# Performer attention and an MLP on one core: loads dealt in halves, omega on ScalarE's queue, and a few splits moved between VectorE and GpSimd

## The chip, the cores and the metric

The kernel runs on one core of a Trainium2 chip, the other cores idle. The metric is the device time of one execution in microseconds. Before and after are compared by the median of several executions; the profile comes from one more execution, whose own time is given below.

## The reference

```python
scale = 1.0 / np.sqrt(np.sqrt(D))             # D = 64; batch 8, heads 8, seq 576, 128 features
def phi(x):
    h = np.einsum('bhsd,md->bhsm', x, omega) - np.sum(x * x, -1, keepdims=True) / 2
    return np.exp(h - h.max(-1, keepdims=True)) / np.sqrt(m)
q_p, k_p = phi(q * scale), phi(k * scale)
kv, z = einsum('bhsm,bhsd->bhmd', k_p, v), k_p.sum(2)
attn = einsum('bhsm,bhmd->bhsd', q_p, kv) / (einsum('bhsm,bhm->bhs', q_p, z)[..., None] + 1e-6)
x = attn.transpose(0, 2, 1, 3).reshape(8, 576, 512)
u = x + (x.transpose(0, 2, 1) @ U @ V).transpose(0, 2, 1)      # mixing along the sequence, rank 32
out = u + np.maximum(u @ w_ch1, 0) @ w_ch2                     # 512 -> 2048 -> 512
```

U, V and the two weights are 64-bit floats, and the kernel decodes them on the chip. The 4608 rows of u make nine chunks of 512.

## The kernel before, in words

**Attention** runs in 16 rounds of 9 steps. Rounds come from 16 units of two batches by two heads; from round 1 on a round has two parts, one of keys and one of queries, and one step handles 128 positions of both. Each part needs a tile `kt` or `qt` of 128 by 1152 numbers, loaded in eight DMAs of 72 KB: `load(0)` brings the first half (four DMAs), `load(1)` the second. A part is turned by VectorE in three transposes of 384 columns (`turn`, L643, one per three steps), split into a high part on ScalarE (`high`, L647) and a remainder on GpSimd (`low`, L651), then projected on TensorE in three matmuls (L771 to L773). VectorE takes the maxima (`peak`, L779), ScalarE the exponentials (L786). TensorE then adds keys into `p_kv` (L683), or transposes queries (L709), which are copied out (`eT`, L714) and multiplied with `kv` (L729, L722). The program is written as a loop over steps with delays by stage (`DELAY`); a scheduler orders each engine's instructions, except where `keep_in_program_order` (K) fixes them.

All loads but a few stand on SyncE's queue, SP. Queue SP takes them in order. At the start omega comes through GpSimd's queue (tile `once`), is scaled and transposed (L838, L840) and split into `omh` and `oml`, without which no projection begins. Twelve matmuls on a tile of zeros (L819) stand on TensorE at the start.

**The decoder** (`decoding`) runs beside the attention and turns U, V and w_ch1 into 32-bit floats: ScalarE (L141, L144), three instructions on VectorE (L159, L160, L163, the `slots`) and an addition on GpSimd (L184). For each half of a group of w_ch1, `Half` then makes four sums (L269) and splits seven operands into high and low parts (L273, L278) for a seven-product matrix scheme; groups 0 and 1 are made during the attention on GpSimd, groups 2 and 3 later.

**Mixing** (`mixing`) runs beside the attention for three pairs of batches and after it for the last: rows are split on ScalarE and GpSimd (L427, L429) and multiplied (L474, L442).

**The MLP** starts inside the last mixing: `early` prepares chunk 0 of u, `guest` chunk 1 (transposes L598, sums L531, splits L536 and L540), and `unit` issues the seven products (L1028), with additions on VectorE (L1014) between them. `BEGIN`, `PACE` and two tuples in the loop over `begun` say at which places the other work is dealt in. The second matmul of the MLP (L1409) follows from about 674 us to the end.

## Time and profile before

| | us |
|---|---|
| three timed executions | 1023.04, 1036.34, 1041.23 |
| their median | 1036.34 |
| the profiled execution | 1022.2 |
| its span, first to last instruction | 1020.3 |
| TensorE busy in the span | 1002.5 |
| VectorE, ScalarE, GpSimd busy | 844.5, 614.6, 516.2 |
| mean granted clock of TensorE | 0.997 |

Busy time is the time in which an engine has an instruction under way. A busy TensorE is not TensorE at its peak: a matmul's record covers its latency, and matmuls overlap. The profiled execution lies beside the fastest of the timed ones.

### The profile page before, as it was taken

Reading aid. Unit: us, or ns where it says so; the run is one execution under the profiler, and the core shown is the slowest. Engines: PE = TensorE matmul, PEld = TensorE weight load, DVE = VectorE, ACT = ScalarE, POOL = GpSimd, SP = SyncE. Lnnn points to the kernel's source line nnn. Section 1 sums busy time; section 2 is a strip of 40 time slices with the busy share of each in tenths; the row PEclk is TensorE's granted clock in tenths of the full one; section 3 lists DMA queues with packets and bytes.
Section 4 is the critical chain, followed back from the end, with each engine's and each line's share of the span. In section 5 each row is a group of like instructions: output and inputs, shape, how many; then the busy total and the mean of one; then the engine's idle time right before and its main releaser. Section 6 shows DMA issues by size and latency. Waiting matters only on the chain.

```text
span 1020.3 us, 23875 instructions
## 1 busy us (share of the span) xinstructions
PE 1002.5 (98%) x8497; PEld 980.9 (96%) x8497; DVE 844.5 (83%) x1507; ACT 614.6 (60%) x1483; POOL 516.2 (51%) x453
## 2 busy tenths in 40 slices
PE   8999999999999999999999999999999999999998
PEld 7899999999997999999999999999999999999998
DVE  4699898898899796766567565779999999999995
ACT  5889989989885557446355354665444454454442
POOL 4446966867536353323415314525756646646543
PEclk9899999999999999999999999999999999999999
DMA  7688588587444785888679768874555455455451
GB/s 141 137 164 157 115 197 161 112 188 145 88 105 113 214 202 144 225 243 207 179 204 238 183 178 273 258 234 155 176 169 204 146 176 177 145 176 176 145 177 51
DMA packets 380518, 175.51 MB, mean 172 GB/s; under 512 B 275552, under 2 KB 353376, under 8 KB 375920
## 3 DMA queue, kind: packets, MB, share of 16 engines
q1 hardware_dynamic: 378000, 173.67, 64.3%
q8 instruction: 67, 1.10, 0.5%
q10 hardware_dynamic: 2368, 0.30, 0.2%
q14 instruction: 51, 0.42, 0.1%
q0 software_dynamic: 32, 0.03, 0.0%
HBM read 109.97 MB, written 63.96 MB: 170 GB/s over the span
## 4 chain that ended last, share of the span: by engine, by line
PE 58%; DMA 1%; DVE 0%; issue 0%; ACT 0%; DVEq 0%
PE p_q L1409 10%; PE p_p L1409 10%; PE p_n L1409 7%; PE p_n L1028 7%; PE p_p L1028 5%; PE p_q L1028 5%; PE p_kv L1409 5%; PE p_kv L1028 4%; PE p_m L1028 3%; PE p_m L1409 2%; DMA raw<-in_moe_w_ch_dram 1%; DVE g L1014 0%; DMA g<-g 0%; ACT g L1010 0%; DVE u L1334 0%
## 5 line engine op out<-in xcount | busy, mean ns | idle before, releaser
L786 ACT ACTIVATE e<-p_p,nm 128x128 f32<-128x128 f32 x576 | 166.4, 397 | 24.9 <-DVE nm L779 15.9
L1247 ACT CAST gh<-gs 128x512 fp32r<-128x512 f32 x140 | 86.8, 623 | 150.4 <-DVE gs L1219 82.9
L1219 POOL TENSOR_TENSOR gs<-graw 128x512 f32<-128x512 f32 x66 | 108.5, 1654 | 125.2 <-DMA graw<-g 72.0
L1010 ACT ACTIVATE g<-g 128x512 f32<-128x512 f32 x105 | 66.4, 634 | 148.0 <-DVE g L1014 91.7
L651 POOL TENSOR_TENSOR xl<-xT,xh 128x384 fp32r<-128x384 f32 x96 | 97.5, 1033 | 99.9 <-ACT xh L647 82.8
L1254 DVE TENSOR_TENSOR gl<-gs,gh 128x512 fp32r<-128x512 f32 x140 | 132.9, 955 | 7.7 <-ACT gh L1247 6.8
L779 DVE TENSOR_REDUCE nm<-p_p 128x4 f32<-128x512 f32 x144 | 98.1, 683 | 27.4 <-ACT e L786 10.3
L184 POOL TENSOR_TENSOR wf<-wf,low 128x512 int32<-128x512 int32 (+2 forms) x35 | 44.0, 1257 | 130.0 <-ACT g L1010 71.8
L771 PE MATMUL p_p<-omh,xh 128*128 128x256 f32 x288 | 93.2, 324 | 1.9 <-ACT e L786 1.6
L1334 POOL TENSOR_TENSOR u<-u,p 128x256 f32<-128x256 f32 x72 | 80.9, 1153 | 24.8 <-DVE u L1334 22.4
L1254 DVE TENSOR_TENSOR gl<-graw,gh 128x512 fp32r<-128x512 f32 x107 | 83.1, 800 | 3.1 <-ACT gh L1247 3.1
L772 PE MATMUL p_p<-oml,xh 128*128 128x256 f32 x288 | 81.5, 283 | 0.0
L773 PE MATMUL p_p<-omh,xl 128*128 128x256 f32 x288 | 81.4, 283 | 0.0
L1409 PE MATMUL p_p<-wh,gh 128*128 128x256 f32 x288 | 79.5, 276 | 0.0
L1409 PE MATMUL p_p<-wl,gh 128*128 128x256 f32 x288 | 79.5, 276 | 0.0
L1409 PE MATMUL p_p<-wh,gl 128*128 128x256 f32 x288 | 79.5, 276 | 0.0
L1247 ACT CAST gh<-graw 128x512 fp32r<-128x512 f32 x107 | 63.7, 621 | 25.6 <-PE p_n L1409 4.9
L1409 PE MATMUL p_q<-wh,gl 128*128 128x256 f32 x276 | 76.3, 276 | 0.0
L1409 PE MATMUL p_q<-wh,gh 128*128 128x256 f32 x276 | 76.2, 276 | 0.0
L1409 PE MATMUL p_q<-wl,gh 128*128 128x256 f32 x276 | 76.2, 276 | 0.0
L729 PE MATMUL p_n<-kv,eT 128*128 128x65 f32 x512 | 73.2, 272 | 2.9 <-ACT eT L714 1.9
L729 PEld LDWEIGHTS p_n<-kv,eT 128*128 128x128 f32 x512 | 68.3, 194 | 6.2 <-ACT eT L714 2.4
(291 smaller groups left out, 3935.8 us busy)
## 6 DMA issues: line engine op xcount, KB each, us to landing
g<-g SPq DMA_DIRECT2D x282, 128.0 KB, 2.6
graw<-g SPq DMA_DIRECT2D x35, 1024.0 KB, 5.2
raw<-in_moe_w_ch_dram SPq DMA_DIRECT2D x23, 512.0 KB, 4.7
u_dram<-ut SPq DMA_DIRECT2D x36, 256.0 KB, 2.5
u<-u_dram SPq DMA_DIRECT2D x36, 256.0 KB, 2.6
out_dram<-u SPq DMA_DIRECT2D x36, 256.0 KB, 2.5
kt<-in_k_dram SPq DMA_DIRECT2D x120, 72.0 KB, 2.5
qt<-in_q_dram SPq DMA_DIRECT2D x120, 72.0 KB, 2.5
```

The costliest lines, as they stand in the source:

```text
L651: nc.gpsimd.tensor_tensor(out=self.xl[-1], in0=self.turned, in1=f32(self.xh[-1]), op=ALU.subtract)
L729: nc.tensor.matmul(pn[:, h, :], eT[:, h, :], kv[:, h, s // 5, :], start=True, stop=True)
L771: nc.tensor.matmul(o, part.xh[g][:, ts], oh, start=True, stop=False)
L772: nc.tensor.matmul(o, part.xh[g][:, ts], ol, start=False, stop=False)
L773: nc.tensor.matmul(o, part.xl[g][:, ts], oh, start=False, stop=True)
L779: nc.vector.tensor_reduce(out=self.nm[:, :n], in_=self.pp[:, :n], axis=AX.X, op=ALU.max, negate=True)
L786: nc.scalar.activation(out=self.e[:, j, :], in_=self.pp[:, j, :], func=AF.Exp, bias=self.nm[:, j : j + 1])
L1028: K(nc.tensor.matmul(p[:, f, :], x[:, k, fs], y[:, k, :], start=first, stop=(k == 1 and y is ul), skip_group_check=True,))
L1219: K(engine.tensor_tensor(out=to, in0=self.val[x], in1=self.val[y], op=op))
L1247: K(nc.scalar.copy(out=h, in_=v))
L1254: K(nc.vector.tensor_tensor(out=l, in0=v, in1=f32(h), op=ALU.subtract))
L1409: K(nc.tensor.matmul(acc[bank][:, half, :], x[:, ks], y[:, f, :], start=(now.s == 0 and k == 0 and half == 0 and x is h and y is wh), stop ...
```

## The change

It does six things. Omega is loaded through ScalarE's queue, ahead of everything else there, and three of the four first-half loads of the second key part follow it on that queue (four of four stood there before); the fourth goes to SP. From round 2 on, the first halves of keys and queries are issued before the second halves. In round 0, the second transpose of the second part stands after the step's maxima. Eight GpSimd instructions on weights (the first sum and one early split of each half of groups 0 and 1) are made to wait for the decoder's latest VectorE slot. Some splits and sums change engine: split 3 of groups 2 and 3, splits 4 and 6 and one sum of `guest` go from VectorE to GpSimd, split 2 of `early` and one row split of the last mixing go from GpSimd to VectorE. And the tables that deal the MLP's other work change a little.

```diff
+    ahead_of = []
+    def behind(inst):
+        if ahead_of:
+            tc.add_manual_dep(
+                inst.ins, ahead_of.pop().ins.name,
+                mybir.DependencyInfo(mybir.DependencyClass.Sync, mybir.DependencyReason.SCHED_ONLY),
+            )
+        return inst
...
-                    tc.keep_in_program_order(slot())
+                    step = tc.keep_in_program_order(slot())
+                    if j < 2 and i < fine < 99:
+                        ahead_of[:] = [step]
...
-            self.sums.tensor_tensor(out=to, in0=self.v[x], in1=self.v[y], op=op)
+            made = self.sums.tensor_tensor(out=to, in0=self.v[x], in1=self.v[y], op=op)
+            if self.sums is nc.gpsimd:
+                behind(made)
...
-            engine = nc.vector if self.g >= EARLY_GROUPS and (0, 1, 0, 1, 0, 1, 0)[i] else self.lows
+            engine = nc.vector if self.g >= EARLY_GROUPS and (0, 1, 0, 0, 0, 1, 0)[i] else self.lows
...
-                rest = nc.vector if last and t not in (0, 1, 2, 3, 4, 5, 6, 7) else nc.gpsimd
+                rest = nc.vector if last and t not in (1, 2, 3, 4, 5, 6, 7) else nc.gpsimd
...
-                (queue or nc.sync).dma_start(
+                (nc.scalar if 2 * h + a < aside else nc.sync).dma_start(
...
-    nc.gpsimd.dma_start(out=once, in_=omega)
+    nc.scalar.dma_start(out=once, in_=omega)
+    keys[0].load(0)
+    keys[1].load(0, 3)
+    for p in keys:
+        p.load(1)
     nc.vector.memset(warm, 0.0)
     K(nc.scalar.activation(out=warm, in_=warm, func=AF.Exp))
-    keys[0].load(0)
-    keys[1].load(0, nc.scalar)
-    for p in keys:
-        p.load(1)
...
                 new[0].load(0)
-                if r:
-                    new[0].load(1)
             if t == 1:
                 new.append(Queries(r + last, 1))
                 new[1].load(0)
                 if r == 0:
                     for p in keys[:2]:
                         p.load_values(1, "t")
-                    new[0].load(1)
+                new[0].load(1)
                 new[1].load(1)
...
-                0, ahead, first, lows=(VE, VE, G_, G_, G_, G_, G_,), sums=(VE, G_, VE, VE,), ...
+                0, ahead, first, lows=(VE, VE, VE, G_, G_, G_, G_,), sums=(VE, G_, VE, VE,), ...
...
-    BEGIN = (3, 5, 6, 9, 11, 13, 14, 16, 17, 18, 19)
+    BEGIN = (3, 5, 6, 8, 11, 13, 14, 16, 17, 18, 19)
-    guest = prepare(1, ..., lows=(VE, VE, VE, VE, VE, VE, VE,), pool=tp, sums=(VE, G_, G_, G_,))
+    guest = prepare(1, ..., lows=(VE, VE, VE, VE, G_, VE, G_,), pool=tp, sums=(G_, G_, G_, G_,))
-    PACE = {2: (0, 1, 1, 0, 1, 2, 1), 3: (3, 3, 3, 3, 5, 3, 0), 4: (2, 1, 2, 1, 2, 4, 2), 5: (1, 1, 2, 1, 1, 1, 2)}
+    PACE = {2: (0, 1, 1, 0, 1, 2, 1), 3: (3, 3, 4, 3, 5, 3, 0), 4: (1, 1, 2, 1, 2, 4, 2), 5: (2, 1, 1, 1, 1, 1, 2)}
...
-        for _ in range((1, 1, 1, 1, 1, 1, 1)[i]):
+        for _ in range((1, 1, 1, 2, 1, 1, 1)[i]):
```

On the queue SP, the loads issued during round 1 (keys of unit 3 and queries of unit 1 for round 2, then the loads of V, values, and the loads for round 3) stood so before:

```order
L623 DMA kt<-in_k_dram 32x18x32 x8
L623 DMA qt<-in_q_dram 32x18x32 x8
L382 DMA raw<-in_moe_V_dram 32x576 x4
L665 DMA vt_134<-in_v_dram 128x4x64 x2
L670 DMA vm_135<-in_v_dram 64x2x64
```

and stand so after (line 638 is line 623 of before, L397 is L382, L680 is L665, L685 is L670):

```order
L638 DMA kt<-in_k_dram 32x18x32 x4
L638 DMA qt<-in_q_dram 32x18x32 x4
L638 DMA kt<-in_k_dram 32x18x32 x4
L638 DMA qt<-in_q_dram 32x18x32 x4
L397 DMA raw<-in_moe_V_dram 32x576 x4
L680 DMA vt_134<-in_v_dram 128x4x64 x2
L685 DMA vm_135<-in_v_dram 64x2x64
```

The four first-half loads of the queries moved ahead of the four second-half loads of the keys; what follows them is in the same order.

On ScalarE at the start of the program, the rows before were these (the tile `qt` holds the second key part here):

```order
L623 DMA qt<-in_k_dram 32x18x32
L811 ACT_TABLE_LOAD
L811 ACTIVATE warm<-warm 128x1
L623 DMA qt<-in_k_dram 32x18x32 x3
L843 CAST omh<-p_q 64x128 x2
```

and are these after:

```order
L824 DMA once<-in_omega_dram 128x64
L638 DMA qt<-in_k_dram 32x18x32 x3
L830 ACT_TABLE_LOAD
L830 ACTIVATE warm<-warm 128x1
L858 CAST omh<-p_q 64x128 x2
```

Omega took the first place, one key load left for SP, where it stands fifth, and the table load moved behind the DMAs.

On GpSimd in round 4 of the attention, where the first half of weight group 0 is made, with each row's semaphore waits (`ml` is a split of the mixing, `xl` a remainder of the attention), the rows before were:

```order
L184 TENSOR_TENSOR wf<-wf,low 128x512 [waits DVE_49]
L269 TENSOR_TENSOR ws<-wf 128x256 [waits Pool_49]
L429 TENSOR_TENSOR ml<-x,mh 128x512 [waits Activation_49]
L269 TENSOR_TENSOR wf<-wf 128x256 [waits Pool_49]
L269 TENSOR_TENSOR ws<-ws,wf 128x256
L429 TENSOR_TENSOR ml<-x,mh 128x512 [waits Activation_49]
L651 TENSOR_TENSOR xl<-xT,xh 128x384 [waits PE_49,Activation_49] x2
```

and after (L195 is L184, L444 is L429, L666 is L651, L280 is L269):

```order
L195 TENSOR_TENSOR wf<-wf,low 128x512 [waits DVE_49]
L444 TENSOR_TENSOR ml<-x,mh 128x512 [waits Activation_49] x2
L666 TENSOR_TENSOR xl<-xT,xh 128x384 [waits PE_49,Activation_49] x2
L280 TENSOR_TENSOR ws<-wf 128x256 [waits DVE_49,Pool_49]
L444 TENSOR_TENSOR ml<-x,mh 128x512 [waits PE_49,Activation_49]
L280 TENSOR_TENSOR wf<-wf 128x256 [waits Pool_49]
L280 TENSOR_TENSOR ws<-ws,wf 128x256
```

The first sum of the weights moved behind two splits of the mixing and two of the attention, and it waits for VectorE now. Eight such waits are new on GpSimd: one at the first sum and one at an early split of each of four halves.

## Rows read from the trace of the kernel before

**Rows 1.** Stretches of the span; by engine busy us and (instructions), granted clock, DMA share.

```profile
100.00:200.00 100.00, 98.89 (x813) 94.20 (x811) 89.89 (x218) 92.46 (x297) 80.81 (x83) 1.00 0.72 149
...
300.00:400.00 100.00, 96.38 (x767) 91.54 (x765) 86.87 (x160) 59.36 (x132) 48.44 (x43) 1.00 0.66 163
400.00:460.00 60.00, 59.04 (x512) 58.49 (x511) 40.27 (x61) 29.31 (x52) 18.35 (x15) 1.00 0.84 228
...
700.00:800.00 100.00, 100.00 (x885) 100.00 (x884) 99.18 (x140) 44.19 (x80) 63.13 (x46) 1.00 0.50 166
```

**Rows 2.** Waits of TensorE: who waited for whom, us in total, times, longest.

```profile
PE p_n L729 <- ACT eT L714: 1.9, 3, 1.2
...
PE py L474 <- POOL ml L429: 1.4, 3, 0.9
...
PE p_n L1028 <- DVE g L1014: 1.1, 2, 0.8
PE p_kv L1028 <- DVE g L1014: 0.9, 1, 0.9
```

**Rows 3.** Timeline around 42 us: start, us, engine, instruction, [idle before, releaser].

```profile
38.00 4.22 SPq L623 DMA_DIRECT2D qt<-in_q_dram  x8
...
39.24 0.15 DVE L739 TENSOR_SCALAR rec<-p_n 128x4 f32<-128x4 f32 x1
...
42.14 0.58 DVE L643 STREAM_TRANSPOSE xT<-qt 128x384 f32<-128x384 f32 x1 [2.74 <-DMA qt<-in_q_dram]
...
43.59 0.66 PE L729 MATMUL p_n<-kv,eT 128*128 128x65 f32 x4 [1.23 <-ACT eT L714]
...
45.66 1.12 PE L729 MATMUL p_n<-kv,eT 128*128 128x65 f32 x4 [0.51 <-DVE eT L714]
```

**Rows 4.** Stretches around the same place, columns as in rows 1.

```profile
42.00:44.40 2.40, 1.01 (x8) 0.73 (x6) 2.26 (x7) 1.19 (x4) 0.99 (x1) 0.99 0.80 143
44.40:51.20 6.80, 6.28 (x28) 5.91 (x29) 4.47 (x12) 5.37 (x18) 3.54 (x4) 0.50 0.68 146
51.20:60.00 8.80, 8.80 (x83) 8.80 (x81) 8.18 (x19) 6.62 (x24) 1.97 (x2) 1.00 0.71 116
```

**Rows 5.** Maxima on VectorE, one per step: ns min/median/max, first and last start.

```profile
L779 DVE TENSOR_REDUCE nm<-p_p x144: 652/691/693, 12.2 to 307.5; 128x4 f32<-128x512 f32 x144
```

**Rows 6.** The queue SP, timeline: two rows of its first 60 us.

```profile
32.48 5.42 SPq L623 DMA_DIRECT2D kt<-in_k_dram  x8
...
52.61 5.68 SPq L623 DMA_DIRECT2D qt<-in_q_dram  x8
```

**Rows 7.** The tile qt until 60 us: ns to issue a load, us to its landing.

```profile
L623 SPq DMA_DIRECT2D qt<-in_q_dram x24: 443/496/1901, 14.6 to 57.8; - x24
...
DMA to landing us min/median/max: 2.2/2.4/4.2
```

**Rows 8.** Timeline of the start, columns as in rows 3.

```profile
0.75 0.43 ACTq L623 DMA_DIRECT2D qt<-in_k_dram  x1
...
1.27 0.68 POOL L809 DMA_DIRECT2D once<-in_omega_dram  x1 [0.81 <-POOLq L1460]
...
4.67 0.30 DVE L838 TENSOR_SCALAR om<-once 128x64 f32<-128x64 f32 x2 [2.65 <-DMA once<-in_omega_dram]
...
6.82 0.58 DVE L643 STREAM_TRANSPOSE xT<-kt 128x384 f32<-128x384 f32 x1
```

**Rows 9.** Splits of line L278 by engine, 300 to 440 us: ns min/median/max.

```profile
L278 POOL TENSOR_TENSOR wl<-wf,wh x14: 737/742/1187, 348.3 to 400.4; 128x256 fp32r<-128x256 f32 x14
...
L278 DVE TENSOR_TENSOR wl<-ws,wh x6: 410/421/1284, 349.4 to 390.7; 128x256 fp32r<-128x256 f32 x6
```

**Rows 10.** Splits of line L540 on VectorE, 300 to 440 us, columns as in rows 9.

```profile
L540 DVE TENSOR_TENSOR wl<-uT,wh x4: 685/692/926, 341.1 to 347.4; 128x512 fp32r<-128x512 f32 x4
```

**Rows 11.** Timeline at 319 us, two splits that began together.

```profile
319.31 5.74 POOL L540 TENSOR_TENSOR ul<-x,uh 128x512 fp32r<-128x512 f32 x4 [1.02 <-ACT uh L536]
319.36 1.80 DVE L540 TENSOR_TENSOR u<-x,u 128x512 fp32r<-128x512 f32 x1
```

More of the change, by code (lines that the diff above doesn't have):

```diff
@@ L276, in low @@
             h, l = (x[:, self.half, :] for x in operand(self.g, i))
-            engine = nc.vector if self.g >= EARLY_GROUPS and (0, 1, 0, 1, 0, 1, 0)[i] else self.lows
-            K(engine.tensor_tensor(out=l, in0=self.v[LEFT[i]], in1=f32(h), op=ALU.subtract))
+            engine = nc.vector if self.g >= EARLY_GROUPS and (0, 1, 0, 0, 0, 1, 0)[i] else self.lows
+            made = K(engine.tensor_tensor(out=l, in0=self.v[LEFT[i]], in1=f32(h), op=ALU.subtract))
+            if engine is nc.gpsimd:
+                behind(made)
             ready.add((self.g, self.half, i))
@@ L614, in performer_mlp_kernel, with blocks @@
     ))
-    def blocks(src, raw, unit, j, queue=None):
+    def blocks(src, raw, unit, j, aside=0):
         pair, hp = unit
@@ L634, in __init__, with load @@
             self.xh, self.xl = [], []
-        def load(self, j, queue=None):
-            blocks(self.src, self.raw, self.unit, j, queue)
+        def load(self, j, aside=0):
+            blocks(self.src, self.raw, self.unit, j, aside)
         def turn(self):
@@ L895, in performer_mlp_kernel @@
             early = prepare(
-                0, ahead, first, lows=(VE, VE, G_, G_, G_, G_, G_,), sums=(VE, G_, VE, VE,), temps=lambda: next(aside).rearrange("p (k t) -> p k t", k=2)
+                0, ahead, first, lows=(VE, VE, VE, G_, G_, G_, G_,), sums=(VE, G_, VE, VE,), temps=lambda: next(aside).rearrange("p (k t) -> p k t", k=2)
             )
@@ L912, in performer_mlp_kernel @@
                 p.copy(st.s)
-        for st in at("turn1"):
-            for p in st.group(1):
-                p.turn()
+        if s != G:
+            for st in at("turn1"):
+                for p in st.group(1):
+                    p.turn()
         for st in at("exp1"):
@@ L955, in performer_mlp_kernel @@
             st.peak()
+        if s == G:
+            for p in steps[s].group(1):
+                p.turn()
         for st in at("combine"):
@@ L1096, in performer_mlp_kernel @@
     guest_raws = loads(1, tp)
-    guest = prepare(1, next(guest_raws), place=lambda i: w_slot(NG - 1, i + 2), lows=(VE, VE, VE, VE, VE, VE, VE,), pool=tp, sums=(VE, G_, G_, G_,))
+    guest = prepare(1, next(guest_raws), place=lambda i: w_slot(NG - 1, i + 2), lows=(VE, VE, VE, VE, G_, VE, G_,), pool=tp, sums=(G_, G_, G_, G_,))
     for n, _ in enumerate(mixers[0]):
```

## The prediction

> **What bounds the kernel now.** I read the busy shares by stretch first [rows 1]. From the middle of the MLP on, TensorE is busy in every microsecond (100.00 of 100 from 700 to 800), and the change touches nothing there, nor the count of real matmuls anywhere. So a gain can only come from places ahead of 460 us where TensorE is idle or slow. The whole span has 1020.3 - 1002.5 = 17.8 us of idle TensorE. The attention (12 to 307 us) is tight on three engines at once: of the 100 us from 100 on, TensorE is busy 98.89, ScalarE 92.46 and VectorE 89.89, GpSimd 80.81. From 300 to 400 TensorE idles 3.62 us and from 400 to 460 0.96.
>
> Then the list of TensorE's waits [rows 2]: none is large. The longest is 1.2 us, and the timeline shows where [rows 3]: VectorE had finished its last ready instruction at 39.24 + 0.15 = 39.39 and stood 2.74 us until the first half of a query tile had landed, at 42.14; all that is queued behind that transpose came late, and TensorE stood 1.23 us and soon after 0.51. The third view is the granted clock [rows 4]: right after this stop, from 44.4 to 51.2, it is 0.50, the lower of the two levels (1.2 GHz), and 1.00 ahead of it and behind. In those 6.8 us TensorE got 28 matmul records done, against 83 in the next 8.8.
>
> What made the loads late is the queue SP [rows 6, 7]. A load of 72 KB takes 0.50 us to issue and 2.4 us to land, and SP had no pause: eight loads of keys from 32.48 took 5.42 us (one issue among them was long), then eight of queries began at 38.00. The transpose needs only the first four of those.
>
> The Trainium skill speaks of this in "DMA: Bandwidth & Descriptors" (Issuing engines are not separate DMA queues): DMAs of all issuing engines run on the same 16 engines, and issuing on several saves only the time of issuing, which it calls usually small beside the transfer. The trace agrees in kind and differs in size: the sixteen loads cost SP 16 x 0.50 = 8 us per round, and here that is what the transpose waits for, while the DMA engines are at 0.80 in that stretch [rows 4].
>
> **The change part by part.**
>
> *Omega and the first loads.* Omega was issued at 1.27 on GpSimd and used at 4.67, 3.4 later [rows 8]. It now goes first on ScalarE's queue, at 0.75, and with the landing times of the loads, 2.4 to 3.4, it is there at 3.2 to 4.2: 0.5 to 1.5 earlier. Behind it stand the scaling, a transpose, two splits and then the first transpose of keys at 6.82, so that one moves up by as much unless its data are not there yet. I take 0.9. ScalarE's other three loads move down by one issue (0.5), and one load more goes to SP: everything on SP is 0.5 us later from then on. That price counts, since SP has no pause up to round 3.
>
> *Halves first.* The first half of the queries now needs eight issues after 32.48 + 0.5 = 32.98, the four of keys and its own. Eight take between 4.22 [rows 3] and 5.42 us [rows 6], so the last begins 0.5 before 37.2 or 38.4 and lands 2.4 later: 39.1 to 40.3 in place of 42.14. VectorE would be ready at 39.4 - 0.9 = 38.5, so it still waits 0.6 to 1.8 us, and what TensorE gains by then is the smaller of two things: 1.8 to 3.0 earlier data, or the start's 0.9 and its own two stops of 1.74, 2.6 together. Start and halves together give 1.8 to 2.6; I take 2.1. They must not be added up, because both run into the same queue. The keys' second half lands four issues later than before, about 41.2 to 42.4. It is needed three steps after the first, a step being (307.5 - 12.2) / 143 = 2.07 us [rows 5], so at about 45: covered by some 3 us.
>
> *The clock.* The low level follows right behind the two stops, 1.74 us together, and there is no second such stretch in the recorded clock: the mean of 0.997 leaves 0.003 x 1020.3 = 3.1 us of lost clock in the whole span, about this one's half of 6.8. I take it that with most of the stops gone it does not come. At full clock TensorE would need 3.4 us less (half of 6.8), but ScalarE has 5.37 us of work in that stretch [rows 4], so the bound on the other side is 6.8 - 5.37 = 1.4. I take 2.1, nearer to ScalarE's end, as ScalarE is next to full in this stage [rows 1]; nothing if the clock falls all the same.
>
> *The second transpose of round 0 behind the maxima.* It lets the first maxima begin one transpose (0.58) earlier and delays the part's second group by the same, which is not needed for two steps. Nothing, hidden by TensorE's warm-up matmuls.
>
> *GpSimd's weight sums.* Eight instructions now wait for VectorE, and the splits of mixing and attention that stood behind the sums stand ahead of them. What it can give is small: TensorE waited 1.4 us in three times for the mixing's splits, 0.9 of it in one [rows 2], so 0.5 is my bound. What it can cost: everything behind a waiting instruction on GpSimd, `ml` for the mixing and `xl` for the projections, waits too, up to one step, 2.07 us, eight times. GpSimd's pause of 19 us in 100 [rows 1] is the cover. I take zero, and the ends are -0.5 and the rival's price below.
>
> *Splits between VectorE and GpSimd, and the tables.* VectorE loses three operations of 128x512 at 0.69 [rows 10] and four of 128x256 at 0.42 [rows 9], 3.8 us, and gets two of the large size, 1.4 us: net 2.4 us less between 300 and 400, where it is busy 86.87 of 100. GpSimd gets the seven and is busy 48.44 there. TensorE's waits on VectorE here are 1.1 and 0.9 us [rows 2]; half of that, 1.0, is my value, between 2.0 and a loss of 2 from moved decoder work.
>
> Where VectorE and GpSimd split side by side, both rows have tails: a VectorE split beside a GpSimd one took 1.80 us in place of 0.69 [rows 11], and a small one 1.28 at the most in place of 0.42 [rows 9]. The Trainium skill has the rule in "SBUF — State Buffer" (Who interferes with whom): a VectorE instruction with two SBUF inputs and a GpSimd one that reads SBUF cannot run together, the later one waits for the other's end. By that rule, with which these rows agree, moving splits to GpSimd costs VectorE time as well as saving it; what that makes of the time is a rival below.
>
> **Sum.** 2.1 (start and halves) + 2.1 (clock) + 1.0 (MLP's opening) = 5.2 us. Against the profiled execution's 1022.2 this gives 1017.0. That execution lies at the low end of what the kernel does: with the three timed ones it makes 1022.2, 1023.04, 1036.34 and 1041.23, with a median of 1029.7. The timed median of the changed kernel I put 5.2 below that: 1024.5.
>
> **Rivals.** First, *the queue stays the bound* (0.2): the order is changed but SP, half a microsecond later, lets a second half or a later round's first half come late, and another stop with its slow clock appears there. For it speaks that SP still issues without pause until 58.3 [rows 6]; against it the 3 us of cover. Then only the 1.0 of the opening is left: 1028.7. Second, *the splits collide* (0.08): three GpSimd splits hold a VectorE one up by 1.80 - 0.69 = 1.11 each and four by 0.86, 6.8 us; less the 2.4 saved and two such collisions that go, 2.2, VectorE is 2.2 us later in the opening and TensorE with it: -4.2 + 2.2 = -2.0, so 1027.7. That is where the skill's rule would lead. Third, the one on the slow side, *GpSimd stands at its new waits* (0.07): each holds it for a step less the sum that it would have done, 2.07 - 0.74 = 1.33 us; eight are 10.6 us, all passed on through `xl` and `ml`, less the 5.2 gained: 5.4 slower, 1035.1. It decides above 0.65 us per wait. Fourth, *the long executions go* (0.05): 1036.34 is 14.1 above the profiled one, about four low-clock stretches of 3.4 us; if such stretches make them and the change prevents them all, the median is 1017.
>
> **How the numbers follow.** The forecast has 0.6. Its own range is 1013 to 1037: a gain of 9 (3.0 + 3.4 + 2.0 and 0.5) on the fastest execution, and a gain of 0 on 1036.34. The other cases lie inside, so the range is 1013 to 1038, with a microsecond for the third. A measurement of this kernel can tell about 2% from no change, here 20.7 us; no case reaches that from the same base, and only a change of the executions' mix could: faster by more than that 0.06, within it 0.92, slower 0.02.
>
> **What would show it.** Right: no wait of VectorE on a query load over 1.8 us, granted clock 1.00 from 40 to 55, the first key transpose near 5.9, the attention's last maxima near 303 (307.5 before), the second matmul of the MLP starting some 5 us earlier. Wrong: a clock of 0.50 somewhere else in the attention, waits of TensorE on `xl` or `ml` above 5 us in total, or VectorE's splits L278 and L540 with longer means and TensorE idle over 4.6 us between 300 and 460.

## The result, and the profile after

The changed kernel takes 1035.36 us (median of six executions, 1034.38 to 1052.39), the kernel before 1025.08 (six, 1022.02 to 1041.23). The ratio is 1.0115 with a 95% interval of 1.008 to 1.0151: slower by 1.2%, some 12 us, where 5 us less were forecast. All ratios here leave out executions more than 1.5% above the fastest of their kernel. The profiled execution after has 1035.95 us and a span of 1033.9; the one before had 1022.2 and 1020.3.

Lines have moved down by 9 to 17 in the changed kernel: the decoder's first step on VectorE is L168 (L159 before), the splits of weights L291 (L278), the MLP's additions L1031 (L1014).

Stretches of the changed kernel, columns as in [rows 1]; they answer to [rows 1, 4]:

```profile
100.00:200.00 100.00, 94.17 (x759) 89.98 (x760) 87.64 (x206) 87.03 (x282) 73.48 (x77) 0.97 0.70 144
300.00:400.00 100.00, 92.56 (x716) 88.62 (x716) 82.27 (x159) 57.89 (x137) 48.63 (x43) 0.95 0.64 158
...
44.40:51.20 6.80, 6.61 (x52) 5.84 (x52) 5.43 (x16) 6.45 (x23) 3.54 (x4) 1.00 0.70 152
82.30:85.80 3.50, 3.50 (x20) 3.50 (x20) 2.27 (x5) 2.22 (x7) 0.79 (x1) 0.51 0.98 211
123.30:130.10 6.80, 4.90 (x22) 4.73 (x23) 4.49 (x8) 1.52 (x6) 1.14 (x1) 0.50 0.16 35
324.70:331.50 6.80, 6.24 (x20) 4.69 (x21) 6.48 (x10) 3.95 (x8) 2.85 (x2) 0.50 0.73 160
382.70:386.10 3.40, 2.99 (x14) 3.00 (x15) 2.92 (x8) 1.49 (x3) 0.34 (x1) 0.50 0.20 60
```

The half clock of [rows 4] is gone from 44.4 to 51.2, as forecast, and TensorE does 52 matmuls there, against 28. But four new stretches at 0.50 have come, 20.5 us in all (before: 6.8), and TensorE does 759 matmuls from 100 to 200 instead of 813, and 716 instead of 767 from 300 to 400. The list of TensorE's waits says what stands ahead of each (answering to [rows 2]):

```profile
PE p_kv L1045 <- DVE g L1031: 5.0, 2, 4.6
PE p_n L744 <- DVE x L769: 4.5, 1, 4.5
...
PE p_n L744 <- ACT eT L729: 2.8, 2, 2.4
PE ph L457 <- DVE ut L465: 2.0, 1, 2.0
...
PE py L489 <- POOL ml L444: 0.6, 1, 0.6
```

Four waits of 2.0 to 4.6 us, none of which was in [rows 2], where the longest had 1.2. The waits on GpSimd's `ml` fell from 1.4 to 0.6. The start and the old stop, timeline (answering to [rows 3, 8]):

```profile
2.83 0.30 DVE L853 TENSOR_SCALAR om<-once 128x64 f32<-128x64 f32 x2 [0.83 <-DMA once<-in_omega_dram]
...
5.50 0.58 DVE L658 STREAM_TRANSPOSE xT<-kt 128x384 f32<-128x384 f32 x1
...
40.57 0.58 DVE L658 STREAM_TRANSPOSE xT<-qt 128x384 f32<-128x384 f32 x1 [2.02 <-DMA qt<-in_q_dram]
```

The first transpose of keys moved from 6.82 to 5.50 and the late transpose of queries from 42.14 to 40.57. The maxima, in one row (answering to [rows 5]):

```profile
L794 DVE TENSOR_REDUCE nm<-p_p x144: 650/691/693, 11.0 to 315.5; 128x4 f32<-128x512 f32 x144
```

They begin 1.2 us earlier and end 8.0 later. To see where, I subtract starts: the same matmul (counted by its tiles) in a kernel less that in before, at places named by the time that it has in before, in us. (I read it at 62 and not at 60, where one group of matmuls has another place in TensorE's order in six of these kernels.) The names are those of the experiments below.

```
kernel                        10    30    62   100   150   300   312   332   362   400   460   690
the changed kernel          -1.5   0.8  -2.3   1.0   7.5   7.8   6.5   9.9   8.5  13.7  12.2  13.7
e1  loads                   -1.5   0.7  -2.8   1.0   1.0   1.2   1.2   1.2   1.0   1.0   1.3   2.2
e2  waits                    0.0   0.2  -2.1  -2.1   4.0   5.3   5.3   5.2   5.4   5.3   4.7   6.3
e3  dealing                 -0.2   0.5  -2.0  -1.5   4.0   5.0   3.7   6.7   5.6  12.0  10.8  13.0
e4  changed, no waits       -1.5   1.0  -2.3   1.6   1.5   1.8   0.4   3.7   2.4   6.1   5.5   7.7
e5  halves later            -1.5  -0.2  -2.4  -2.8   3.5   5.9   4.5   8.1   6.7  10.5   9.6  10.4
e6  next waits              -1.5   8.8   3.0   3.1   4.8   5.7   4.3   7.5   6.4  10.1  10.5  12.7
e7  three engine entries     0.1   0.3  -1.0  -0.9  -0.9  -0.9  -2.2   1.5   0.3   0.5  -0.4   0.6
e8  other four entries       0.0   0.2   0.4   0.4   0.4   0.4   0.4   0.1  -0.6   3.2   2.4   3.2
e9  next waits, round 2     -1.5   1.0  -2.3   2.3   3.9   4.8   3.5   7.4   5.9   8.8   7.8   9.1
e10 mended                  -1.5  -0.9  -3.3  -3.3  -1.6  -0.7  -0.7  -0.8  -0.1   0.0  -1.1   0.7
e11 guest's engines          0.0   0.4   0.5   0.5   0.4   0.4   0.5   0.4  -0.6   1.5   1.1   3.1
e12 tables                   0.1   0.1   0.0   0.0  -0.1  -0.1   0.0  -0.4  -0.5   2.8   2.7   3.7
e13 changed again           -1.5   1.0  -2.1   1.2   7.7   8.0   6.7  10.1   9.0  12.9  12.5  13.9
e14 no waits again          -1.5   1.6  -1.8   2.2   7.8   8.1   6.8  10.2   8.9  13.8  14.2  14.9
e15 loads, halves later     -1.5  -0.5  -2.8  -2.8  -2.9  -1.8  -1.8  -1.9  -1.6  -1.6  -2.1   1.3
e16 as e15, with waits      -1.5  -0.5  -2.7  -3.0   4.2   5.5   5.5   5.4   5.2   5.2   5.5   6.2
e17 one number of PACE       0.2   1.0  -2.1  -1.3  -1.4  -1.4  -1.4  -1.4  -1.6  -0.3  -1.2  -0.8
e18 change mended           -1.5   0.2  -3.2  -3.2  -3.3  -2.3  -2.3  -2.6  -3.3  -1.3  -2.9  -2.2
```

In the changed kernel the start gains 1.5, and 3.1 are gained from 30 to 62, where the old stop lay. The losses are 2.3 ahead of 30, 3.3 from 62 to 100, 6.5 from 100 to 150, 3.4 from 312 to 332 and 5.2 from 362 to 400. Three of the four stops, read in the timeline of the changed kernel:

*At 77 us* (start, us, engine, instruction, idle before and what ended it), two rows of before and then the changed kernel:

```profile
71.67 0.43 SPq L213 DMA_DIRECT2D raw<-in_moe_w_ch_dram  x1
...
78.75 0.69 ACT L141 ACTIVATE wf<-raw 128x512 f32<-128x512 f32 x1
```

```profile
69.78 3.04 SPq L638 DMA_DIRECT2D qt<-in_q_dram  x4
72.92 0.43 SPq L224 DMA_DIRECT2D raw<-in_moe_w_ch_dram  x1
...
78.69 0.66 ACT L150 ACTIVATE wf<-raw 128x512 f32<-128x512 f32 x1 [2.01 <-DMA raw<-in_moe_w_ch_dram]
...
79.80 0.36 ACT L729 COPY eT<-p_q 128x256 f32<-128x256 f32 x1
...
80.21 0.66 PE L744 MATMUL p_n<-kv,eT 128*128 128x65 f32 x4 [2.37 <-ACT eT L729]
```

The decoder's next load of w_ch1 (`raw`) stands in SP's queue behind sixteen loads of keys and queries. It stood so in before, and SP began the sixteen at the same time there (62.91, now 63.08) and came to the raw load at 71.67. But TensorE is 2.3 us ahead at 62 us, and SP is not: the raw load is issued 1.25 us later than in before and lands at 78.67 (76.18 before). ScalarE's first instruction on the raw data stands ahead of the copy `eT`, and TensorE needs that copy. The lead alone does not make the stop: e2, e3 and e17 of the experiments below load in the old order and are 2.0 to 2.1 us ahead at 62 us; the load lands there at 77.06 to 77.46, and ScalarE waits 0.3 to 0.7 us for it. In the six profiles with the new order and this stop (the changed kernel, e1, e4, e9, e13, e14) it lands at 78.02 to 79.23, and ScalarE waits 1.9 to 2.3.

*At 120 us*, VectorE, GpSimd and TensorE:

```profile
119.32 0.77 POOL L291 TENSOR_TENSOR wl<-wf,wh 128x256 fp32r<-128x256 f32 x1
...
119.47 5.25 DVE L168 TENSOR_SCALAR wf<-wf 128x512 f32<-128x512 f32 x1
...
120.01 1.31 POOL L444 TENSOR_TENSOR ml<-x,mh 128x512 fp32r<-128x512 f32 x1
...
121.24 1.98 POOL L666 TENSOR_TENSOR xl<-xT,xh 128x384 fp32r<-128x384 f32 x2
...
123.14 1.30 POOL L444 TENSOR_TENSOR ml<-x,mh 128x512 fp32r<-128x512 f32 x1
124.64 0.91 DVE L769 TENSOR_TENSOR x<-p_n,rec 128x256 f32<-128x256 f32 x3
125.20 1.08 PE L744 MATMUL p_n<-kv,eT 128*128 128x65 f32 x4 [4.51 <-DVE x L769]
```

A decoder step, 0.42 us long where nothing disturbs it, takes 5.25: as long as GpSimd goes from one instruction to the next without a break. It ends 0.28 us after GpSimd's last (123.14 + 1.30).

*At 378 us*, two rows of SP in before, and then SP, ScalarE and VectorE in the changed kernel:

```profile
362.99 2.24 SPq L1004 DMA_DIRECT2D g<-g  x2
365.33 1.47 SPq L213 DMA_DIRECT2D raw<-in_moe_w_ch_dram  x1
```

```profile
375.17 1.26 SPq L1021 DMA_DIRECT2D g<-g  x1
...
376.52 0.41 SPq L224 DMA_DIRECT2D raw<-in_moe_w_ch_dram  x1
...
376.99 4.03 SPq L1021 DMA_DIRECT2D g<-g  x7
...
381.86 0.66 ACT L150 ACTIVATE wf<-raw 128x512 f32<-128x512 f32 x1 [3.98 <-DMA raw<-in_moe_w_ch_dram]
382.36 0.69 DVE L1031 TENSOR_TENSOR g<-p_kv,u 128x512 f32<-128x512 f32 x1 [4.24 <-DMA g<-g]
```

A raw load now stands between the two halves of a shift of g (`g<-g`), for which VectorE waits 4.24 us; TensorE idles 4.64.

### The profile page after: what moved, and what is told of

Its sections match the earlier page's. It is cut to its first block, busy times and chain, and to the rows that moved or that the text cites. A ratio compares the mean times of both kernels' runs of the same rounds, so it can differ in the third digit from the quotient of the medians.

```text
span 1033.9 us, 23873 instructions
## 1 busy us (share of the span) xinstructions
PE 1006.8 (97%) x8497; PEld 985.0 (95%) x8497; DVE 844.3 (82%) x1502; ACT 613.5 (59%) x1483; POOL 517.3 (50%) x457
## 4 chain that ended last, share of the span: by engine, by line
PE 82%; ACT 4%; DMA 4%; DVE 4%; issue 2%; SPq 2%; POOL 1%; DVEq 0%; ACTq 0%; POOLq 0%
PE p_p L1426 9%; PE p_q L1426 9%; PE p_n L1045 9%; PE p_n L1426 7%; PE p_p L1045 7%; PE p_q L1045 6%; PE p_kv L1426 4%; PE p_kv L1045 4%; PE p_m L1045 4%; PE p_n L744 4%; PE p_kv L698 4%; PE p_p L786 3%; PE p_p L788 2%; PE p_p L787 2%; PE p_q L724 2%; PE p_m L1426 2%
## 5 line engine op out<-in xcount | busy, mean ns | idle before, releaser
L666 POOL TENSOR_TENSOR xl<-xT,xh 128x384 fp32r<-128x384 f32 x96 | 97.2, 1028 | 105.5 <-ACT xh L662 71.4
L195 POOL TENSOR_TENSOR wf<-wf,low 128x512 int32<-128x512 int32 (+2 forms) x35 | 44.0, 1257 | 133.4 <-ACT g L1027 72.4
```

The source lines that it names most:

```text
L666: nc.gpsimd.tensor_tensor(out=self.xl[-1], in0=self.turned, in1=f32(self.xh[-1]), op=ALU.subtract)
```

## The experiments

Times are medians of 6 to 12 executions; each ratio is to the kernel before on the same chip. A stop of TensorE is counted here from the start of one matmul to the start of the next, 0.3 to 0.4 us more than the idle time in the rows above. The theories are: L, the order of the loads brings the attention's stops; W, GpSimd's new waits do; D, the new dealing brings the late ones. Q, T, G and C come up on the way.

**One part alone.**

e1, the diff's changes to omega, `blocks`, `new[0].load(1)` and the turn at `s == G`, and nothing else. 

> The kernel before with the change to the start and to the order of the query and key loads alone (omega first on ScalarE's queue, first halves of both new operands ahead of second halves, the one transpose moved behind the maxima); GpSimd's waits and the new dealing of the MLP are left as before. Theory L (the loads' order shifts the rounds so that new stops arise in the attention): the stop at 42 us goes and those at 77 and 120 us of the changed kernel are here too: about 6 us longer than before, 1031, with a VectorE decoder step of over 3 us near 120. Theory W (GpSimd's new waits bunch its work in front of VectorE) and theory D (the dealing) expect the gain alone, about 2.5 us less than before, 1022 to 1023, no low clock after 60 us in the attention.

1025.92 us, ratio 1.0023 (0.999 to 1.0056). L for the stop at 77 (2.54 us, here at 77.02), not for that at 120: the step near 119 takes 1.21 us. The loads gain 3.5 us between 30 and 62 and lose 3.8 by 100. The time is neither the 1031 of L nor the 1022 to 1023 of the others.

e2, the eight waits alone:

```diff
+                    if j < 2 and i < fine < 99:
+                        ahead_of[:] = [step]
...
+            if self.sums is nc.gpsimd:
+                behind(made)
```

> The kernel before with GpSimd's eight new waits in the attention alone. Theory W: a VectorE decoder step stands beside a train of GpSimd's instructions for 3 to 5 us at one place or more, a stretch at half clock follows, 5 to 8 us longer than before. Theories L and D: within 2 us of before, 1023 to 1027, TensorE's stop at 42 us as before.

1029.9 us, ratio 1.0061 (1.002 to 1.0103). As W: a step of 5.06 us at 116.54, a stop of 4.88, half clock behind it, 6.1 us lost from 100 to 150.

e3, the seven entries of the dealing alone (`lows` of `early`, the mixing row, `low`, `BEGIN`, `guest`, `PACE`, the chores). 

> The kernel before with the new dealing of the MLP's weight work alone (seven table entries). Theory D: TensorE's stop of over 4 us in the first MLP group (at 378 us in the changed kernel, some 369 here) and a stretch at half clock behind it, and VectorE's additions at the end of the attention meet GpSimd's and half clock follows: 4 to 6 us longer than before, 1029 to 1031. Theories L and W, by which the two late stops come from the shift that the attention hands on: within 2 us of before.

1028.05 us, ratio 1.0022 (0.9986 to 1.0059). As D, both late stops are here: 2.40 us at 319 and 4.91 at 375. But W got a blow too: without any wait, and with GpSimd's and VectorE's instructions up to 300 us in the order of before, the step at 116.51 takes 5.09 us.

e4, the changed kernel without the waits:

```diff
-                    if j < 2 and i < fine < 99:
-                        ahead_of[:] = [step]
```

> The changed kernel without GpSimd's eight new waits. Theory W: the 5.25 us decoder step at 119 us is gone, with the 6 us that round 6 loses there: 1028 to 1030. Theory L: the stops at 77 and 120 us stay, 1034 to 1036. Theory D: 378 stays in either case.

1029.34 us, ratio 1.0038 (1.0007 to 1.007). As W: the step takes 1.25 us, nothing is lost from 100 to 150; the stop at 77 (2.98) and the late ones (2.40, 3.33) stay.

**One stop mended.**

e5, the changed kernel with second halves two steps later:

```diff
+            if t == 3:
                 new[0].load(1)
                 new[1].load(1)
```

> The changed kernel, with the second halves of both operands issued two steps later, so that the decoder's next raw load stands ahead of them in SP's queue. Theory Q (that load lands late because eight second halves stand ahead of it): the 2.65 us stop at 77 us and ScalarE's 2.0 us wait on the raw load go, the clock is full at 82 us, and round 4 begins some 4 us earlier than in the changed kernel; over the whole 1029 to 1031 if the decoder step at 119 us is held as before. Rival (the transfer itself is slow beside the other loads): the stop stays and the time is within 1.5 us of 1034.6.

1032.23 us, ratio 1.0053 (1.0019 to 1.0087). As Q. ScalarE and TensorE at the old stop, and then the stretch (the changed kernel has 35 matmuls there at a clock of 0.79):

```profile
76.33 0.70 ACT L150 ACTIVATE wf<-raw 128x512 f32<-128x512 f32 x1
...
77.91 0.66 PE L744 MATMUL p_n<-kv,eT 128*128 128x65 f32 x4 [0.31 <-ACT eT L729]
```

```profile
78.00:86.00 8.00, 7.83 (x71) 7.62 (x71) 6.94 (x20) 6.76 (x25) 2.06 (x3) 1.00 0.69 132
```

ScalarE no longer waits for the load, and round 4 is 3.8 us ahead of the changed kernel at 100 us (-2.8 against 1.0). The step at 115.68 is held again, 5.23 us.

e6, the changed kernel with the wait on GpSimd's next instruction, whichever it is (the same edit also in `mixing`):

```diff
-            nc.gpsimd.tensor_tensor(out=self.xl[-1], in0=self.turned, in1=f32(self.xh[-1]), op=ALU.subtract)
+            behind(nc.gpsimd.tensor_tensor(out=self.xl[-1], in0=self.turned, in1=f32(self.xh[-1]), op=ALU.subtract))
```

> The changed kernel, with the wait on the decoder's step put on GpSimd's very next instruction (low parts of operands and of the mixing rows too) and not on the next weight sum. Theory T (VectorE's step gets in only where GpSimd's row of ready instructions has a break): no decoder step over 3 us in the attention, round 7 begins 5 to 6 us earlier than in the changed kernel, 1028 to 1030. Theory G (a GpSimd that stands and falls behind is itself what costs): TensorE waits over 2 us for GpSimd's low parts, 1035 or more.

1037.02 us, ratio 1.0114 (1.005 to 1.0177). Both theories, at different places. At 120 T: the step takes 2.10 us and only 1.7 us are lost from 100 to 150. In round 1 G; GpSimd's timeline:

```profile
30.40 2.02 POOL L668 TENSOR_TENSOR xl<-xT,xh 128x384 fp32r<-128x384 f32 x2 [11.99 <-DVE wf L168]
```

It stood 12 us behind a decoder step that itself waited for its first load; TensorE stopped 4.70 us, and half clock followed.

e7, before with the mixing row 0 and the two weight parts on other engines (`early`, `low`). 

> The kernel before with three of the seven entries of the dealing: the mixing row and the two weight parts whose engine changes (row 0 from VectorE to GpSimd, one early low part from GpSimd to VectorE, one late low part from VectorE to GpSimd). If the stop of 2.4 us at 322 us comes from these: it is here near 316 to 320, with VectorE's 128x512 additions at 1.6 us beside GpSimd, 1.5 to 3.5 us longer than before; the 4.9 us stop in the first MLP group is not here. If both stops come from the MLP's pace: neither is here, within 1 us of before.

Row 0 goes the other way than I wrote there: its split moves from GpSimd to VectorE, as the diff has it.

1025.06 us, ratio 0.9996 (0.9951 to 1.0041). The stop of 2.40 us is here, at 313, and the 4.9 us one is not (1.24). Against before it gains 1.3 us from 300 to 312, loses 3.7 by 332 and gains 1.2 by 362, a net loss of 1.2, and the time does not show the 1.5 to 3.5 us expected. In the changed kernel the same place looks like this (VectorE and GpSimd):

```profile
320.29 1.64 DVE L546 TENSOR_TENSOR x<-x 128x512 f32<-128x512 f32 x1
321.94 1.28 POOL L444 TENSOR_TENSOR ml<-x,mh 128x512 fp32r<-128x512 f32 x1 [0.56 <-ACT mh L442]
...
322.11 1.65 DVE L546 TENSOR_TENSOR x<-x 128x512 f32<-128x512 f32 x1
```

With row 0's split on VectorE, GpSimd's splits of the next rows fall beside both of these sums of VectorE, 1.64 and 1.65 us in place of 0.68; in before the second one fell between two of GpSimd's splits and took 0.68. TensorE then waits 2.02 us for VectorE. Of the three entries it is row 0, since the splits that the other two move come later, and e18 below, which keeps the early one's move and not row 0's, has no such stop.

e8, before with the other four entries. 

> The kernel before with the other four entries: the start of the MLP's products, the guest group's engines, the pace table and the chores. If the 4.9 us stop of the first MLP group comes from these: it is here near 370 and costs 4 to 6 us, 1028 to 1030, with no 2.4 us stop near 320. Otherwise within 1 us of before.

1027.77 us, ratio 1.0028 (0.9975 to 1.008). A stop of 3.06 us at 369, 3.8 us lost from 362 to 400; none of 2.4 near 320.

e9, the changed kernel with e6's waits from round 2 on:

```diff
+            if len(rounds) > 3:
+                behind(made)
```

> The changed kernel with the wait on GpSimd's very next instruction again, but from round 2 on alone, so that round 1 has no instruction of GpSimd behind a decoder step that itself waits for its load. Theory T: the 4.7 us stop at 27 us and the half clock behind it are gone, the decoder step near 119 us takes under 2.5 us, TensorE's stop there under 2 us; 5 us less than the changed kernel, 1029 to 1030. Theory G: 1034 or more, because GpSimd's waits cost TensorE elsewhere.

1030.82 us, ratio 1.0103 (1.0042 to 1.0163). T in the trace; GpSimd, VectorE and TensorE at 121 us:

```profile
120.75 2.07 DVE L168 TENSOR_SCALAR wf<-wf 128x512 f32<-128x512 f32 x1
...
121.26 1.28 POOL L444 TENSOR_TENSOR ml<-x,mh 128x512 fp32r<-128x512 f32 x1
...
122.97 1.97 POOL L668 TENSOR_TENSOR xl<-xT,xh 128x384 fp32r<-128x384 f32 x2 [0.43 <-DVE wf L168]
...
123.30 0.63 PE L748 MATMUL p_n<-kv,eT 128*128 128x65 f32 x4 [1.36 <-DVE x L773]
```

As soon as GpSimd stands, 0.43 us for this very step, the step is done. 1.6 us are lost from 100 to 150 instead of 6.5. The ratio, though, is hardly below the changed kernel's on another chip, so what this saves over the whole is not settled by it.

e10, the loads of e1, second halves later, e9's waits, the dealing of before. 

> The change to start and loads, second halves two steps later, waits on GpSimd's next instruction from round 2 on, the dealing of before. If the stops at 77 and 119 us and the dealing are all that made the change long: 1 to 3 us less than before, 1021 to 1024. If another stop takes their place: 1026 or more.

1021.81 us, ratio 0.9987 (0.9955 to 1.0018). No stop above 1.8 us and no half clock after the start; the median is as expected, the gain on before is within the measurement.

e11 and e12, the dealing's `guest` entry alone, and `BEGIN`, `PACE` and chores alone. 

> The kernel before with the guest group's engines alone dealt anew (two low parts and one sum from VectorE to GpSimd). If GpSimd's share makes the stop of 3 to 5 us near 370: it is here, 1027 to 1029. If the pace tables make it: not here, within 1 us of before.

 

> The kernel before with the start of the products, the pace table and the chores alone as in the changed kernel. If these make the stop near 370: it is here, 3 us or more, 1027 to 1029. If the guest group's engines make it: not here, within 1 us of before.

e11: 1023.4 us, ratio 1.0007 (0.9977 to 1.0036), two stops of 1.46 and 1.76 near 369 and 380. e12: 1024.98 us, ratio 1.0026 (0.9995 to 1.0058), a stop of 2.70 at 369, then half clock, 3.3 us lost from 362 to 400. So the tables make the stop with half clock behind it. The guest's engines are not cleared, for e11 loses 2.1 us from 362 to 400 as well, with VectorE waiting 1.87 us for a shift at 374. SP and VectorE in e12:

```profile
362.83 2.08 SPq L1004 DMA_DIRECT2D g<-g  x1
365.01 1.66 SPq L213 DMA_DIRECT2D raw<-in_moe_w_ch_dram  x1
366.72 3.85 SPq L1004 DMA_DIRECT2D g<-g  x7
...
371.29 0.69 DVE L1014 TENSOR_TENSOR g<-p_kv,u 128x512 f32<-128x512 f32 x1 [1.80 <-DMA g<-g]
```

In before both halves of that shift were issued ahead of the raw load (the two rows of before shown for 378 us).

**Waits or chance.** After e3 it was open whether the waits, or the moment alone (theory C), let the step be held. Two pairs on one chip:

e13, the changed kernel once more, and e14, e4 once more. 

> The changed kernel itself, with a second profile. Theory W (the waits make the step fall into a closed row of GpSimd's instructions in every execution): the step near 119 us takes about 5.2 us again, and the time is 5 us above the form without waits. Theory C (chance of the moment): the step may as well take 1.2 us, and the times of the two forms overlap.

 

> The changed kernel without the eight waits, on the same chip as the changed kernel. Theory W: the step near 119 us takes about 1.2 us again, and the fast executions are 5 us below those of the changed kernel. Theory C: overlapping times, the step taking 1.2 or 5 us.

e13: 1043.72 us, ratio 1.016 (1.01 to 1.022), the step 5.23. e14: 1034.94 us, ratio 1.0065 (1.0025 to 1.0104), the step 5.09 in its profile. The shortest execution of e13, 1035.57, lies 5 us above the five shortest of e14.

e15, the loads with second halves later and nothing else, and e16, the same with the eight waits. 

> The change to start and loads alone, with second halves two steps later, no waits and the dealing of before. From the drift of the trace with the mended loads (3 us ahead of before at 100 us): 2 to 3 us less than before if the step near 115 us is not held, 2 to 4 us more if it is. Theory W expects it not to be held.

 

> As the last, with GpSimd's eight waits on the weight sums as in the changed kernel. Theory W: the step near 115 us takes about 5.2 us, and it is 4 to 6 us longer than the form without the waits. Theory C: no difference beyond 2 us between the two.

e15: 1028.66 us, ratio 0.9976 (0.9928 to 1.0023), the step 1.25. e16: 1029.62 us, ratio 1.0017 (0.9979 to 1.0056), the step 5.23, and 7.2 us lost from 100 to 150, where e15 loses none. By the ratios 4 us lie between the two, as W has it, but their intervals overlap.

With the waits on the weight sums the step is held 5.06 to 5.25 us in five profiles of five (the changed kernel, e2, e5, e13, e16). Without them it is in two of twelve (e3, e14) and takes 1.21 to 1.25 in the other ten. Had the waits no part in it, all five would be among the seven held ones once in 6188 / 21 = 295 times. The place shows how they act. GpSimd and VectorE in before, and then in e14:

```profile
116.42 2.53 POOL L429 TENSOR_TENSOR ml<-x,mh 128x512 fp32r<-128x512 f32 x2
...
118.00 1.24 DVE L159 TENSOR_SCALAR wf<-wf 128x512 f32<-128x512 f32 x1
...
118.92 0.91 POOL L278 TENSOR_TENSOR wl<-wf,wh 128x256 fp32r<-128x256 f32 x1
```

```profile
118.67 2.53 POOL L429 TENSOR_TENSOR ml<-x,mh 128x512 fp32r<-128x512 f32 x2
...
120.24 5.09 DVE L159 TENSOR_SCALAR wf<-wf 128x512 f32<-128x512 f32 x1
...
121.17 0.72 POOL L278 TENSOR_TENSOR wl<-wf,wh 128x256 fp32r<-128x256 f32 x1
```

Without waits GpSimd does two mixing splits and then a weight split, and the step begins in the second mixing split. In ten profiles it got in between that and the weight split, which ran 0.91 to 0.93 us instead of 0.72; in two it did not, and then not at the boundaries behind it either. With the waits the weight split has changed places with a mixing split, the step begins in the weight split, and it never got in at the boundary behind that. So both W and C hold: the waits set the order, and in the old order the held profiles differ from the others by a few nanoseconds in the step's start (below). That each long execution of the forms without waits has a held step is not shown; e14's profile (1037.14) is one of its two near 1037, its five shortest lie from 1029.13 to 1030.36.

**The last entry, and the rest.**

e17, before with one number of `PACE` (`3: (3, 3, 4, ...`). 

> The kernel before with one number of the pace table changed (3 to 4 in the first MLP group's third row). It puts a raw load ahead of the second half of a shift of g in SP's queue. If that order makes the stop: TensorE stops 2.5 to 3.5 us near 369, VectorE waiting for the shift, 2 to 3 us longer than before over the whole. If the other entries of the tables make it: no stop over 1.5 us near 369, within 1 us of before.

1038.65 us, ratio 1.0045 (0.9987 to 1.0102). A stop of 2.08 us at 368, 1.3 lost from 362 to 400, no half clock behind it. That one number moves the raw load ahead of the shift's second half, and the stop is here; but VectorE did not wait for the shift in this profile, it waited 0.7 for ScalarE's part of the decoder and did two small decoder steps first. So this entry brings a stop, and the wait behind it is not the same each time; that it makes all of e12's 3.3 us is not shown.

e18, the change with all that had been found taken out: second halves later, no waits, the dealing without row 0, the late low part and that one number. 

> The change with the start and loads (second halves two steps later), without GpSimd's waits, with the dealing but for three entries (mixing row 0, the late low part, the one number of the pace table), so that the raw load stands behind the shift as before. If the stops found so far are all that the change cost: no stop over 1.5 us between 60 and 460 us unless VectorE's step near 115 us is held by chance, 1 to 4 us less than before. If the rest of the dealing costs too: no less than before.

1026.69 us, ratio 1.0004 (0.9978 to 1.003). TensorE's largest stop between 60 and 460 us is 1.97, over the 1.5 that I named, and what makes it stays open. The profiled execution has 1020.23, 2.0 less than that of before, but before has one of 1020.22 on this chip. No gain that the times can tell, so whether the rest of the dealing costs too is open.

## Why the prediction was wrong, point by point

*Omega and the first loads:* the first transpose came 1.3 us earlier, not 0.9, and TensorE 1.5. By 30 us that is lost again wherever all new loads go out at once (+0.7 to +1.6); with second halves later the kernels lie between 0.9 ahead and 0.2 behind (e10, e18). Not all of this is the loads' doing: kernels that load as before lie 0.1 to 1.0 behind there.

*Halves first and the clock:* right in place and near in size, but the size is mostly luck. The old stop and its half clock are gone, 3.1 us from 30 to 62, against 2.1 for both edits less the start's 0.9, and 2.1 for the clock: 3.3. But the base was no fixed thing: e2, e3 and e17, which load in the old order, gain 2.3 to 3.1 us on the profile of before at this place, because no half clock followed, and at 62 us they are within 0.3 us of the changed kernel. In five of the eight profiles with the old order half clock follows this stop (before, e7, e8, e11, e12); in none of the twelve with the new order is there any half clock between 40 and 60 us. So the new order is worth something here, but the forecast priced the bad case as if it came each time. *The second transpose of round 0* was put at nothing; no run takes it alone.

*What comes late next* was a step that I passed over. I gave the first rival, that the queue stays the bound and another stop appears, 0.2, and priced it as a gain forgone. It happened at 77 us, and not through a key or query load, which I had counted, but through the decoder's load behind them: TensorE had come forward, and that load landed later, not earlier. That took back 3.3 us (62 to 100), and with eight loads moved behind the raw load (e5) nothing is lost there.

*"GpSimd's weight sums ... I take zero"* is the step that failed most, by 6 us. I asked what stands behind a waiting instruction on GpSimd, and that came out: waits of at most 2.9 us, TensorE waiting less for `ml`. I did not ask what a wait does to the order of the instructions round it, nor what a row of GpSimd's instructions without a break does to VectorE. The third rival had the side and 5.4 us, but by another mechanism, which its own mark (TensorE on `xl` or `ml`) refuted; that its 1035.1 lies beside the measured 1035.36 is luck, since it stood on a base of 1029.7 and the six executions of before gave 1025.08. The second rival had the mechanism and the wrong place: I priced a collision by [rows 9, 11], 0.86 to 1.11 us, as if VectorE waited for one instruction; here it waited for five in a row.

The Trainium skill has the rule for this in "SBUF — State Buffer" (SBUF: two separate sides): of a GpSimd instruction and a VectorE one that runs in a two-port mode or has two SBUF inputs, the one that starts first holds the shared pair of ports for its whole instruction and the other blocks. No run shows in which mode the decoder step runs. The rows agree that the later one waits, and differ in how long: not to the end of that instruction, but past four boundaries between GpSimd's instructions. The measurement decides.

*Splits and tables* were put at a gain of 1.0 and cost 5.9 us in the changed kernel from 300 to 690, of which 1.0 belongs to the loads (e1). I reckoned VectorE's load, 2.4 us less, and from 300 to 460, a stretch that covers most of this work in both, VectorE is busy 125.2 us instead of 127.1. What cost was where the work fell. Row 0's move put GpSimd's splits beside two of VectorE's sums (e7), a stop of 2.4 us that costs 0.7 net by 362; 5.2 came from 362 to 400, where a raw load of 512 KB stands between two halves of a shift (e12, e17) and the guest's engines have a part that is not parted from it (e11). By the timed executions the dealing alone is anything from a gain of 1 to a loss of 6 us (e3).

*The signs.* Of those for right, the clock of 1.00 from 40 to 55 us and the earlier first transpose (5.50, with 5.9 named) came. VectorE's wait on a query load was 2.02 us, over the 1.8 named; the last maxima lie at 315.5, and the second matmul of the MLP begins 12.5 us later than before, at 686.0. Of those for wrong, half clock came elsewhere in the attention, and TensorE idles 7.4 us between 300 and 460, with 4.6 named; its waits on `xl` and `ml` are 0.9 us in total. *The fourth rival* fell: the changed kernel still has executions of 1043.34 and 1052.39, and e15's profiled execution took 1036.56 us with a mean granted clock of 1.000, so no half clock made that one long.

## What to carry to other kernels

Where engines are as full as here, price a reordered queue by the next load in it that an in-order engine touches, not by the one that was late; and look at several profiles before a single stop with its half clock is put on the credit side. Before adding waits on GpSimd or moving work between it and VectorE, look for rows of GpSimd's instructions without a break beside a VectorE instruction on SBUF: that can cost the length of the row, here 5 us, and not of one instruction. Several such stops, each with half clock behind it, can swallow a change whose every part looks like a small gain.

## What the runs showed of the hardware that I had not expected

A VectorE instruction of 0.42 us was held 5.06 to 5.25 us beside GpSimd in seven profiles, past every boundary between GpSimd's instructions, and ended within 0.3 us of the first break. Whether it got in at the first boundary went, in the old order, with when it began in GpSimd's 1.28 us split: 0.313 to 0.355 us after the split's start it got in (ten profiles), 0.307 and 0.309 after it did not (two). That this moment decides is not shown by a run that sets it.

Half clock followed 32 of the 33 stops of 2.4 us or more between 12 and 460 us, and not always for the same time: behind the stop of 2.7 at 77 us 3.4 us of it in the changed kernel, 6.8 in e9; none behind 3.45 at 376 in e9, while two idle times of 1.74 together were followed by 6.8 us in before.

The granted clock alone does not tell TensorE's rate. Stretch of the second matrix stage, in before and in e13:

```profile
800.00:900.00 100.00, 100.00 (x885) 100.00 (x884) 96.99 (x131) 45.84 (x79) 56.28 (x42) 1.00 0.52 170
```

```profile
800.00:900.00 100.00, 100.00 (x852) 100.00 (x851) 93.33 (x128) 44.48 (x76) 49.92 (x41) 1.00 0.49 161
```

TensorE is busy throughout and the granted clock is 1.00 in both, yet 852 matmuls go through instead of 885, 3.7% fewer, and the same from 700 to 1000 us. e2, e15 and e16 have 851 or 852 there too, all other profiles 884 or 885. What slows them is not in the records.
